# Attention outputs of sixteen units summed inside PSUM, with a drain between row halves, and three weight stores moved to SP

## The chip, the core and the metric

The kernel runs on one core of a Trainium2 chip, as one program. The metric is the device time of one execution in microseconds. The engines are TensorE (PE, with its weight loads shown as PEld), VectorE (DVE), ScalarE (ACT), GpSimd (POOL) and SyncE (SP, which here only issues DMAs). ACT can issue DMAs as well.

## The reference, cut to what matters

```
gamma = 1 - 2 ** (-5 - arange(8));  state = 0
for t in range(768):                                   # 4 batches, 8 heads, head size 64
    state = gamma * state + outer(k[t], v[t])          # one 64x64 state per batch and head
    y[t] = q[t] @ state / sqrt(64)
x = y of all heads side by side                        # 3072 tokens x 512
h = x @ w_in; g = h - tanh(h); x = g @ w_out           # 512 -> 2048 -> 512
h = x @ w_in2; solu, layer norm; out = ln @ w_out2     # 512 -> 1024 -> 512
```

The decay is taken out of the recurrence by scaling q and v with tables of powers of gamma, so that a chunk of 128 tokens needs only matrix products: the output of a chunk is (state before it) times q, plus v times the masked scores inside the chunk.

## The kernel before, in words

The tokens are cut into 24 attention units: 6 chunks `c` of 128 tokens times 4 batches `b`, unit k = 4c + b. Four units make a superblock of 512 tokens. Units 0 to 7 come first and alone (the start of the program). Units 8 to 15 are worked between the steps of the first layer on superblocks 0 and 1. Units 16 to 23 come later, inside the next stage.

A unit has two parts. The score part ("sc" in the rows, written for unit `ks`) makes 16 products of keys with queries and then 16 products that update the state, each 64x64; DVE masks the scores (`pr`) and keeps the states (`sb`, `sa`). The output part ("out", for unit `ko`) makes the output: `fr`, state times q, and `y`, v times masked scores. The function `unit(ko, ks)` issues the output part of one unit and then the score part of a later one; in the start loop ks = ko + 2.

TensorE runs 64x64 products in the four quarters of its array: a product whose operands lie in partitions 0 to 63 uses the upper row half, one with operands in 64 to 127 the lower row half. In the kernel before each `y` product goes to a bank chosen by its row half (`y[ab]`), and each `fr` product to the bank of its own row half (`fr[h]`), so that the two halves never write to the same place. The two terms are then added outside: ACT copies `fr` to `xf` in SBUF (lines 295, 298, 299) and DVE adds `y` in one or two operations (line 303). For units 0 to 7 the result is split into a high part `xh` (ACT, line 341) and a low part `xl` (line 342: one half on DVE, the other on POOL; for unit 7 both on DVE). For units 8 to 15 `xf` is kept.

A step of the first layer, `step_h(n, b)`, is 12 products of 128x512 of weight tile n with the split x of superblock b, called step (n, b) below; ACT and DVE then make g = h - tanh(h). The PE order is the order of the code in this part: step (0,0) after the output part of unit 6, step (1,0) after that of unit 7, then (0,1), (1,1), (2,0), (2,1), (3,0) and so on; from n = 3 a call of `unit` follows each pair of steps. The weights arrive as 64-bit words (`raw`, loaded by SP), and ACT and DVE decode them: `wf` on ACT (line 131), four DVE operations (lines 138 to 145), a high part on ACT (line 154) and a low part on DVE (line 155). The decoded tile is also stored to DRAM (`wfd`), at line 185, from ACT's queue. The order inside each engine's stream, where the code does not pin it, is chosen by a scheduler before the program runs; at run time every engine and every DMA queue works strictly in its order.

Of the kernel before, what the change touches and what calls it, by code (L numbers as in the profile page):

```python
# [26 lines left out]
F32 = mybir.dt.float32  # L27
# [3 lines left out]
ALU = mybir.AluOpType  # L31
# [4 lines left out]
B, H, S, D = 4, 8, 768, 64  # L36
P = 128
DM = H * D
NT = B * S
NP = H // 2  # L40
NC = S // P
NU = NC * B
SB = B * P
# [22 lines left out]
def col(p, h):  # L66

    return h ^ (p & 1)
# [22 lines left out]
def body(ctx: ExitStack, tc, z, w_in, w_out, w_in2, w_out2, g_ln, cst, tab, out):  # L91
# [72 lines left out]
    class Decoder:  # L164
# [59 lines left out]
    def rows(h):  # L224
        return slice(h * D, (h + 1) * D)

    def products(todo):
        for o, a, b in todo:
            pin(nc.tensor.matmul(o, a, b, start=True, stop=True, skip_group_check=True), held[0])  # L229

    def prepare(k, own, wide=False, fixed=True):

# [22 lines left out]
            ), wide and fixed)  # L255
        vs[k] = v

    def unit(ko, ks, hold=False, pool=ps_r, tag="r", opool=ps_r, engs=None, amid=None):

        if ko is not None:
            c, b = divmod(ko, B)
            q, v, po, st = qs.pop(ko), vs.pop(ko), pt.pop(ko), (sa.pop(ko, None), sb.pop(ko))
            w = [opool.tile([P, 2, 4 * D], F32, tag="r", name="out") for _ in range(2)]
            fr = [t[:, 0, :].rearrange("q (i t) -> q i t", i=2) for t in w]
            y = [t[:, 1, :].rearrange("q (h i t) -> q h i t", h=2, i=2) for t in w]

            steps = range(2) if c else (1,)  # L270
            products([
                (
                    fr[h][rows(col(2 * i + odd, h)), i, rows(ab)],
                    st[ab][rows(h), 2 * i + odd, :], q[rows(h), 2 * i + odd, rows(ab)],
                )
                for i in range(2) for ab in steps for odd in range(2) for h in range(2)
            ])
            products([
                (
                    y[ab][rows(col(p, h)), h, p // 2, :], v[rows(ab), 2 * p + h, :],  # L280
                    po[rows(ab), h, p, :],
                )
                for p in range(NP) for ab in range(2) for h in range(2)
            ])
            if hold:
                if b == 0:
                    xf_of[c] = xfp.tile([P, 2, 2, SB], F32, tag=f"xf{c % 2}", name="xf")
                xf = xf_of[c][:, :, :, b * P : (b + 1) * P]
            else:
                xf = t2([P, 2, 2, P], F32, "xf")  # L290
            xa = xf.rearrange("q h i t -> q (h i) t")
            ya = [t.rearrange("q h i t -> q (h i) t") for t in y]
            if c:
                for h in range(2):
                    pin(nc.scalar.copy(xf[:, h, :, :], fr[h]), amid)
            else:
                for h in range(2):
                    pin(nc.scalar.copy(xf[:, h, :, rows(1)], fr[h][:, :, rows(1)]), amid)
                pin(nc.scalar.copy(xa[:, :, rows(0)], ya[0]), amid)
            if amid:  # L300
                amid()
            for ab in steps:
                pin(nc.vector.tensor_tensor(
                    xa[:, :, rows(ab)], xa[:, :, rows(ab)], ya[ab], ALU.add
                ), amid)
            if not hold:
                split_x(c, b, xf, engs or (nc.gpsimd, nc.gpsimd), amid)
        if ks is not None:
            c = ks // B
            kt, kv, v, q = zq.pop(ks)[:, 1, :, :], zv.pop(ks), vs[ks], qs[ks]  # L310
            w = [pool.tile([P, 2, 4 * D], F32, tag=tag, name="sc") for _ in range(2)]
            sc, gn = ([t[:, n, :].rearrange("q (p t) -> q p t", p=NP) for t in w] for n in range(2))
            products([
                (sc[h][rows(ab), p, :], kt[rows(h), p, rows(ab)], q[rows(h), p, rows(ab)])
                for p in range(NP) for h in range(2) for ab in range(2)
            ])
            products([
                (gn[ab][rows(h), p, :], kv[rows(ab), 0, p, rows(h)], v[rows(ab), 2 * p + h, :])
                for p in range(NP) for ab in range(2) for h in range(2)
            ])  # L320
            pr = t2([P, 2, NP, D], F32, "pr")
            for h in range(2):
                pin(nc.vector.tensor_tensor(
                    pr[:, h, :, :], sc[h], mask.unsqueeze(1).to_broadcast([P, NP, D]), ALU.mult
                ), amid)
            pt[ks] = pr
            sb[ks] = stp.tile([P, NP, D], F32, tag="sb", name="sb", bufs=3)
            if c == 0:
                nc.scalar.copy(sb[ks], gn[0])
            else:  # L330
                nc.vector.tensor_tensor(sb[ks], sa[ks], gn[0], ALU.add)
            if c < NC - 1:
                sa[ks + B] = stp.tile([P, NP, D], F32, tag="sa", name="sa")
                nc.vector.tensor_tensor(sa[ks + B], sb[ks], gn[1], ALU.add)

    def split_x(c, b, xf, engs, fixed=False):
        if b == 0:
            xt[c] = [[t4([P, 2, SB], F32R, f"x{n}") for _ in range(2)] for n in "hl"]
        for h in range(2):
            xh, xl = (xt[c][n][h][:, :, b * P : (b + 1) * P] for n in range(2))  # L340
            pin(nc.scalar.copy(xh, xf[:, h, :, :]), fixed)
            pin(engs[h].tensor_tensor(xl, xf[:, h, :, :], xh.bitcast(F32), ALU.subtract), fixed)


    def products_h(s, f, pool, tag):
        ph = pool.tile([P, SB], F32, tag=tag, name="ph")
# [257 lines left out]
    def step_h(n, b):  # L604
        if b == 0:
            g2[n] = t4([P, 2, SB], F32, "g")
        less_tanh(products_h(b, n, ps_y, "y"), g2[n][:, b, :])
# [18 lines left out]
            prepare(k, H // 2, True)  # L626

    for k in range(2 * B):
        both = (nc.vector, nc.gpsimd) if k < 2 * B - 1 else (nc.vector, nc.vector)
        unit(  # L630
            k, k + 2 if k + 2 < 2 * B else None, engs=both,
            amid=lambda: ahead(k + 3), **spare
        )
# [12 lines left out]
    gs = {}  # L646

    def split_g(n):
        g = g2.pop(n)
        gs[n] = [split(g[:, b, :], nc.scalar, nc.vector) for b in range(2)]  # L650

    for n in range(NF1):
        while dec1.at[3] < n + 1:
            dec1.step()
        if n == NF1 - 1:
            split_g(0)
        for b in range(2):
            if n > 1 or b:
                step_h(n, b)

        k = 2 * B + n - LATER
        if 2 * B <= k <= 4 * B:
            unit(k - 1 if k > 2 * B else None, k if k < 4 * B else None, True)
# [480 lines left out]
```

## Time and profile before

| | before |
|---|---|
| median of 3 runs (lowest, highest) | 874.56 us (872.98, 876.18) |
| profiled execution | 874.34 us, span 872.6 us, mean TensorE clock 0.992 |
| busy PE, DVE | 838.4 us (96%), 551.0 us (63%) |
| busy ACT, POOL | 438.6 us (50%), 286.6 us (33%) |

Busy time says which engine is nearly full over the whole program; it doesn't say what limits a given stretch. The profiled execution took 1.74 us outside the span of its instructions. In timeline rows the columns are start and length in us, engine, line, operation, tiles and count; brackets give the idle time just before and what ended it. "issue" is a wait for nothing that the profile shows. The trace counts each 64x64 product in f32 as two records.

### The profile page before, as it was taken

Reading aid. Unit: us, or ns where it says so; the run is one execution under the profiler, and the core shown is the slowest. Engines: PE = TensorE matmul, PEld = TensorE weight load, DVE = VectorE, ACT = ScalarE, POOL = GpSimd, SP = SyncE. Lnnn points to the kernel's source line nnn. Section 1 sums busy time; section 2 is a strip of 40 time slices with the busy share of each in tenths; the row PEclk is TensorE's granted clock in tenths of the full one; section 3 lists DMA queues with packets and bytes.
Section 4 is the critical chain, followed back from the end, with each engine's and each line's share of the span. In section 5 each row is a group of like instructions: output and inputs, shape, how many; then the busy total and the mean of one; then the engine's idle time right before and its main releaser. Section 6 shows DMA issues by size and latency. Waiting matters only on the chain.

```text
span 872.6 us, 16582 instructions
## 1 busy us (share of the span) xinstructions
PE 838.4 (96%) x6488; PEld 691.3 (79%) x6488; DVE 551.0 (63%) x1023; ACT 438.6 (50%) x868; POOL 286.6 (33%) x244
## 2 busy tenths in 40 slices
PE   5799999999999988999999999999999999999997
PEld 4678788788877867888788888887788888888886
DVE  3788975999758678224454977566555555555541
ACT  4655644555555546445443445434655555555442
POOL 4411100160624345343300430234644444444200
PEclk8899999999999999999999999999999999999999
DMA  9657754345899617955766456631211111100001
GB/s 365 251 213 280 272 199 138 118 153 181 301 347 346 230 62 234 412 194 176 275 244 207 155 185 217 190 109 48 86 49 49 49 48 48 45 30 25 21 17 48
DMA packets 66462, 144.34 MB, mean 165 GB/s; under 512 B 6608, under 2 KB 19024, under 8 KB 66384
## 3 DMA queue, kind: packets, MB, share of 16 engines
q1 hardware_dynamic: 58032, 128.28, 41.5%
q10 hardware_dynamic: 8352, 15.00, 4.6%
q8 instruction: 51, 0.84, 0.4%
q14 instruction: 27, 0.22, 0.1%
HBM read 94.50 MB, written 48.76 MB: 164 GB/s over the span
## 4 chain that ended last, share of the span: by engine, by line
PE 81%; DVE 8%; DMA 4%; ACT 3%; issue 2%; SPq 1%; POOL 0%; ACTq 0%; POOLq 0%; DVEq 0%
PE py L378 25%; PE po L966 15%; PE ph L739 14%; PE ph L902 13%; PE ph L353 8%; PE out L229 2%; PE ptr L952 2%; DMA z<-z 2%; PE sc L229 2%; DMA raw<-w_in 1%; DVE wcl L162 1%; DMA wod<-wf 1%; DVE wsum L532 1%; DVE hs L765 0%; DVE wf L145 0%
## 5 line engine op out<-in xcount | busy, mean ns | idle before, releaser
L378 PE MATMUL py<-gp,w 128*128 128x512 f32 x768 | 175.6, 389 | 1.6 <-DVE gp L162 1.6
L378 PEld LDWEIGHTS py<-gp,w 128*128 128x128 f32 x768 | 144.0, 188 | 32.3 <-DVE gp L162 2.0
L966 PE MATMUL po<-w,uh 128*128 128x512 f32 x384 | 118.4, 390 | 0.0
L757 POOL TENSOR_TENSOR hs<-hs,th 128x512 f32<-128x512 f32 x48 | 66.5, 1391 | 94.3 <-ACT th L755 81.2
L966 PEld LDWEIGHTS po<-w,uh 128*128 128x128 f32 x384 | 72.0, 188 | 15.0
L353 PE MATMUL ph<-xh,w 128*128 128x512 f32 x256 | 82.2, 395 | 1.1 <-DVE w L155 1.1
L378 PE MATMUL py<-gh,w 128*128 128x512 f32 x256 | 79.3, 390 | 0.3 <-ACT gh L366 0.3
L494 POOL TENSOR_TENSOR yla<-yl,yha 128x512 fp32r<-128x512 f32 (+1 forms) x24 | 34.4, 1453 | 137.4 <-ACT yha L493 137.4
L966 PE MATMUL po<-w,ul 128*128 128x512 f32 x192 | 74.8, 389 | 0.0
L154 ACT CAST w<-wf 128x512 fp32r<-128x512 f32 x70 | 43.0, 620 | 56.8 <-DVE wf L145 48.8
L902 PE MATMUL ph<-w,yhs 128*128 128x512 f32 x192 | 61.2, 400 | 1.0 <-ACT part L909 1.0
L739 PE MATMUL ph<-xh,wch 128*128 128x512 f32 x140 | 56.8, 405 | 5.3 <-DVE hs L765 4.7
L162 DVE TENSOR_TENSOR gp<-g,gp 128x512 fp32r<-128x512 f32 x64 | 49.7, 788 | 18.8 <-ACT gp L161 18.6
L755 ACT ACTIVATE th<-hs 128x512 f32<-128x512 f32 x48 | 30.3, 631 | 55.3 <-DVE hs L765 51.4
L155 DVE TENSOR_TENSOR w<-wf,w 128x512 fp32r<-128x512 f32 x70 | 50.5, 726 | 11.2 <-ACT w L154 10.2
L353 PEld LDWEIGHTS ph<-xh,w 128*128 128x128 f32 x256 | 48.0, 188 | 12.1 <-DVE w L155 1.5
L378 PEld LDWEIGHTS py<-gh,w 128*128 128x128 f32 x256 | 48.0, 188 | 10.6 <-ACT gh L366 0.7
L739 PE MATMUL ph<-xh,wcl 128*128 128x512 f32 x140 | 54.7, 390 | 0.0
L739 PE MATMUL ph<-xl,wch 128*128 128x512 f32 x140 | 54.6, 390 | 0.0
L765 DVE TENSOR_TENSOR hs<-ph,part 128x512 f32<-128x512 f32 x48 | 32.8, 686 | 34.6 <-PE ph L739 20.4
L927 ACT ACTIVATE ex<-hn,nm 128x1024 f32<-128x1024 f32 x24 | 27.7, 1153 | 53.1 <-DVE nm L917 52.1
L739 PE MATMUL ph<-xh,wc 128*128 128x512 f32 x168 | 52.9, 390 | 1.0 <-DVE hs L765 0.8
(124 smaller groups left out, 1771.5 us busy)
## 6 DMA issues: line engine op xcount, KB each, us to landing
z<-z SPq DMA_DIRECT2D x48, 512.0 KB, 6.9
g<-gd SPq DMA_DIRECT2D x64, 256.0 KB, 5.3
raw<-w_in SPq DMA_DIRECT2D x24, 512.0 KB, 6.4
raw<-w_out SPq DMA_DIRECT2D x24, 512.0 KB, 4.4
gd<-hs SPq DMA_DIRECT2D x48, 256.0 KB, 3.2
y1d<-ysb SPq DMA_DIRECT2D x24, 256.0 KB, 3.4
wc<-wcd SPq DMA_DIRECT2D x12, 512.0 KB, 6.9
yl<-y1d SPq DMA_DIRECT2D x12, 512.0 KB, 3.9
```

The lines of the kernel that those rows point to most:

```text
L154: pin(nc.scalar.copy(hi, wf), fixed)
L155: pin(eng.tensor_tensor(lo, wf, hi.bitcast(F32), ALU.subtract), fixed)
L162: eng.tensor_tensor(o, src, h.bitcast(F32), ALU.subtract)
L229: pin(nc.tensor.matmul(o, a, b, start=True, stop=True, skip_group_check=True), held[0])
L353: nc.tensor.matmul(ph, a[:, k, :], x, start=n == 0, stop=n == 3 * NK - 1), s < 2
L378: nc.tensor.matmul(py[e], a[:, cols], x, start=f == 0 and n == 0, stop=f == NF1 - 1 and n == 2)
L494: nc.gpsimd.tensor_tensor(o, src, h.bitcast(F32), ALU.subtract)
L739: nc.tensor.matmul(ph, a, x, start=first and n == 0, stop=n == 5, skip_group_check=True)
L757: eng.tensor_tensor(g, h, th, ALU.subtract)
L765: nc.vector.tensor_tensor(h, ph, part, ALU.add)
L902: nc.tensor.matmul(ph, x[:, r, :], w, start=first and n == 0, stop=n == 5, skip_group_check=True)
L966: nc.tensor.matmul(po, a[:, f, :], b, start=f == 0 and n == 0, stop=f == NF2 - 1 and n == 2)
```

## The change

For units 0 to 15 the output part goes to a new function `outputs`. Both terms of row half h are accumulated in one bank `w[h]`. The products whose operands lie in the bank's own row half (`fr` and half of `y`, `own(0)`) come first. The other half of `y` (`own(1)`) comes from the opposite row half into the same bank, behind a `drain` of TensorE, in `rest`. `unit` issues `rest` between the score products and the state products of the next unit; where there is no next unit (units 6, 7 and 15) it is returned and issued after the following step. ACT and DVE then read the finished sum from PSUM: `xh` and `xl` directly for units 0 to 7, with `xl` always on DVE, and one copy for each half for units 8 to 15. The DVE additions are gone for these units. Units 16 to 23 keep the old way (`outputs_apart`). The stores of weight tiles 0, 1 and 2 go from ACT's queue to SP's.

```diff
-                        pin(nc.scalar.dma_start(out=to, in_=wf), fixed)
+                        (nc.scalar if i > 2 else nc.sync).dma_start(out=to, in_=wf)
...
+    def outputs(ko, pool, amid):
...
+        w = [pool.tile([P, 2, P], F32, tag="r", name="out") for _ in range(2)]
+        steps = range(2) if c else (1,)
+        def own(off):
+            return [
+                (
+                    w[h][rows(col(p, h)), p // 2, rows(h ^ off)], v[rows(h ^ off), 2 * p + h, :],
+                    po[rows(h ^ off), h, p, :], False,
+                )
+                for p in range(NP) for h in range(2)
+            ]
+        products([
+            (
+                w[h][rows(col(2 * i + odd, h)), i, rows(ab)],
+                st[ab][rows(h), 2 * i + odd, :], q[rows(h), 2 * i + odd, rows(ab)],
+                i == 0 and ab == steps[0],
+            )
+            for i in range(2) for ab in steps for odd in range(2) for h in range(2)
+        ] + own(0))
+        def rest(hold):
+            pin(nc.tensor.drain())
+            products(own(1))
+            if not hold:
+                split_x(c, b, w, amid)
+                return
+            for h in range(2):
+                pin(nc.scalar.copy(xf_to(c)[:, h, :, b * P : (b + 1) * P], w[h]), amid)
...
+        return rest
...
     def unit(ko, ks, hold=False, ...):
...
+        products([(sc[h][...], kt[...], q[...]) ...])
+        if rest:
+            rest(hold)
+        products([(gn[ab][...], kv[...], v[...]) ...])
...
+    def split_x(c, b, w, amid):
...
         for h in range(2):
+            pin(nc.scalar.copy(part[h][0], w[h]), amid)
...
+        for h in range(2):
+            pin(nc.vector.tensor_tensor(
+                part[h][1], w[h], part[h][0].bitcast(F32), ALU.subtract
+            ), amid)
...
             step_h(k - (2 * B - 2), 0)
+            rest(False)
...
             if n > 1 or b:
                 step_h(n, b)
+            if later:
+                later(True)
+                later = None
```

The drain has no row of its own in the listings below, which give the order of an engine's instructions without any time.

TensorE, before: the end of step (0,0) (`ph`), the whole output part of unit 7, and the first product of step (1,0).

```order
L353 MATMUL ph<-xh,w 128x512
L229 MATMUL out<-vq,sa 64x64 x4
L229 MATMUL out<-vq,sb 64x64 x4
L229 MATMUL out<-vq,sa 64x64 x4
L229 MATMUL out<-vq,sb 64x64 x4
L229 MATMUL out<-pr,vq 64x64 x16
L353 MATMUL ph<-xh,w 128x512
```

TensorE, changed, at the same place.

```order
L396 MATMUL ph<-xh,w 128x512
L230 MATMUL out<-pr,vq 64x64 x8
L230 MATMUL out<-vq,sa 64x64 x4
L230 MATMUL out<-vq,sb 64x64 x4
L230 MATMUL out<-vq,sa 64x64 x4
L230 MATMUL out<-vq,sb 64x64 x4
L230 MATMUL out<-pr,vq 64x64 x8
L396 MATMUL ph<-xh,w 128x512
```

The first eight products behind step (0,0) are now the second half of unit 6; the second half of unit 7 has moved behind step (1,0), directly ahead of step (0,1), which reads unit 7's `xh` and `xl`.

SP's DMA queue, before, from the 20th entry, with buffer numbers: `tab` are the q tables, `raw` the weight tiles 2 to 6, `z` the input of later units.

```order
L1016 DMA gl_70<-g_ln 128x8
L208 DMA tab_1061<-tab 128x512
L208 DMA tab_1447<-tab 128x512
L125 DMA raw_931<-w_in 128x1024
L125 DMA raw_933<-w_in 128x1024
L125 DMA raw_978<-w_in 128x1024
L125 DMA raw_980<-w_in 128x1024
L125 DMA raw_1016<-w_in 128x1024
```

SP's DMA queue, changed, at the same place.

```order
L1063 DMA gl_70<-g_ln 128x8
L185 DMA wfd0_71<-wf_286 128x512
L208 DMA tab_1029<-tab 128x512
L185 DMA wfd1_72<-wf_386 128x512
L208 DMA tab_1413<-tab 128x512
L125 DMA raw_886<-w_in 128x1024
L125 DMA raw_888<-w_in 128x1024
L185 DMA wfd2_73<-wf_890 128x512
L125 DMA raw_946<-w_in 128x1024
L125 DMA raw_948<-w_in 128x1024
```

The stores of tiles 0 and 1 stand around a table load, and the store of tile 2, which waits until `wf_890` is decoded, stands ahead of the loads of tiles 4 and later.

DVE, changed, just behind the finish of weight tile 2, with buffer numbers: `wf_950`, `wf_952` and `wf_954` are weight tiles 3, 4 and 5, and `w_964` is the finished tile 3.

```order
L138 TENSOR_SCALAR wf_950<-wf_950 128x512
L138 TENSOR_SCALAR wf_952<-wf_952 128x512
L139 TENSOR_SCALAR wf_950<-wf_950 128x512
L139 TENSOR_SCALAR wf_952<-wf_952 128x512
L138 TENSOR_SCALAR wf_954<-wf_954 128x512
L142 SCALAR_TENSOR_TENSOR wf_950<-raw_888,wf_950 128x512
L142 SCALAR_TENSOR_TENSOR wf_952<-raw_946,wf_952 128x512
L139 TENSOR_SCALAR wf_954<-wf_954 128x512
```

Before, tile 3 was taken through lines 138, 139 and 142 ahead of the first operation on tile 4; now operations on tiles 4 and 5 stand between those on tile 3.

## Rows read from the trace of the kernel before

**Rows 1.** The page: busy time, PE by 40 slices, instruction queue (packets, MB, share).

```profile
PE 838.4 (96%) x6488; PEld 691.3 (79%) x6488; DVE 551.0 (63%) x1023; ACT 438.6 (50%) x868; POOL 286.6 (33%) x244
...
PE   5799999999999988999999999999999999999997
...
q8 instruction: 51, 0.84, 0.4%
```

**Rows 2.** Chain of waits, 0 to 200 us: start, length, what.

```profile
65.89 1.09 PE sc L229 x64
...
128.72 16.56 PE ph L353 x72
```

**Rows 3.** PE in order of time, 20 to 41 us.

```profile
22.37 0.38 PE L229 MATMUL sc<-vq,z 64*64 64x64 f32 x3 [1.89 <-issue]
...
28.13 0.50 PE L229 MATMUL out<-vq,sb 64*64 64x64 f32 x13 [2.22 <-ACT sb L329]
...
29.27 2.05 PE L229 MATMUL sc<-vq,z 64*64 64x64 f32 x63
...
35.96 0.27 PE L229 MATMUL out<-vq,sa 64*64 64x64 f32 x1 [1.00 <-issue]
...
40.31 0.27 PE L229 MATMUL out<-vq,sa 64*64 64x64 f32 x2 [2.22 <-issue]
```

**Rows 4.** DMA queues, stretches of 0.2 us from 19.7, 33.5, 37.9 and 103.6 us.

```profile
q8 instruction: 1, 0.02, 33.8%
...
q8 instruction: 1, 0.02, 30.0%
...
q8 instruction: 1, 0.02, 29.8%
...
q8 instruction: 1, 0.02, 30.2%
```

**Rows 5.** ACT in order of time, 20 to 48 us.

```profile
23.01 0.67 ACT L131 ACTIVATE wf<-raw 128x512 f32<-128x512 f32 x1 [1.83 <-DMA z<-z]
...
27.70 0.37 ACT L329 COPY sb<-sc 128x256 f32<-128x256 f32 x1 [0.52 <-DVE pr L323]
...
46.84 0.71 ACT L341 CAST xh<-xf 128x256 fp32r<-128x256 f32 x2 [0.88 <-DVE xf L303]
```

**Rows 6.** DVE in order of time, 45 to 61 us.

```profile
45.99 0.75 DVE L303 TENSOR_TENSOR xf<-xf,out 128x256 f32<-128x256 f32 x2 [0.46 <-ACT xf L295]
47.27 0.76 DVE L342 TENSOR_TENSOR xl<-xf,xh 128x256 fp32r<-128x256 f32 x2 [0.53 <-ACT xh L341]
...
59.87 0.68 DVE L155 TENSOR_TENSOR w<-wf,w 128x512 fp32r<-128x512 f32 x1
```

**Rows 7.** PE in order of time, 45 to 107 us.

```profile
45.20 0.50 PE L353 MATMUL ph<-xh,w 128*128 128x512 f32 x1
...
60.61 0.73 PE L353 MATMUL ph<-xh,w 128*128 128x512 f32 x2 [1.06 <-DVE w L155]
...
106.01 0.46 PE L229 MATMUL sc<-vs,z 64*64 64x64 f32 x16 [0.60 <-issue]
```

**Rows 8.** Line 229, 64 to 130 us: duration in ns, least, median and most.

```profile
L229 PEld LDWEIGHTS out<-pr,vs x256: 135/135/135, 73.0 to 128.5; 64*64 64x64 f32 x128
L229 PE MATMUL out<-pr,vs x256: 218/218/218, 73.1 to 128.5; 64*64 64x64 f32 x128
```

**Rows 9.** DMA issues to 60 us (KB, us to landing), and SP in order of time.

```profile
raw<-w_in SPq DMA_DIRECT2D x8, 512.0 KB, 7.0
...
36.02 3.25 SPq L125 DMA_DIRECT2D raw<-w_in  x5
```

**Rows 10.** Busy time by stretch: PE, PEld, DVE, ACT, POOL, then clock and DMA.

```profile
128.00:150.00 22.00, 22.00 (x146) 18.28 (x136) 12.26 (x22) 8.44 (x16) 0.00 (x0) 1.00 0.42 137
...
160.00:180.00 20.00, 20.00 (x90) 16.55 (x89) 20.00 (x38) 10.61 (x19) 8.54 (x1) 1.00 0.41 132
```

**Rows 11.** Who PE waited for, 200 to 260 us: total, times, longest.

```profile
PE out L229 <- DVE sa L334: 0.9, 1, 0.9
PE ph L739 <- ACT ysb L388: 0.3, 1, 0.3
```

More of the change, by code (lines that the diff above doesn't have):

```diff
@@ L227, in products @@
     def products(todo):
-        for o, a, b in todo:
-            pin(nc.tensor.matmul(o, a, b, start=True, stop=True, skip_group_check=True), held[0])
+        done = []
+        for o, a, b, *first in todo:
+            done.append(nc.tensor.matmul(
+                o, a, b, start=not first or first[0], stop=True, skip_group_check=True
+            ))
+            pin(done[-1], held[0])
+        return done
     def prepare(k, own, wide=False, fixed=True):
@@ L300, in unit @@
             if amid:
                 amid()
[L302 to L334, printed above, removed]
@@ L336, in split_x, with xf_to, outputs_apart @@
-    def split_x(c, b, xf, engs, fixed=False):
+        return rest
+    def xf_to(c):
+        if c not in xf_of:
+            xf_of[c] = xfp.tile([P, 2, 2, SB], F32, tag=f"xf{c % 2}", name="xf")
+        return xf_of[c]
+    def outputs_apart(ko, pool):
+        c, b = divmod(ko, B)
+        q, v, po, st = qs.pop(ko), vs.pop(ko), pt.pop(ko), (sa.pop(ko, None), sb.pop(ko))
+        w = [pool.tile([P, 2, 4 * D], F32, tag="r", name="out") for _ in range(2)]
+        fr = [t[:, 0, :].rearrange("q (i t) -> q i t", i=2) for t in w]
+        y = [t[:, 1, :].rearrange("q (h i t) -> q h i t", h=2, i=2) for t in w]
+        products([
+            (
+                fr[h][rows(col(2 * i + odd, h)), i, rows(ab)],
+                st[ab][rows(h), 2 * i + odd, :], q[rows(h), 2 * i + odd, rows(ab)],
+            )
+            for i in range(2) for ab in range(2) for odd in range(2) for h in range(2)
+        ])
+        products([
+            (
+                y[ab][rows(col(p, h)), h, p // 2, :], v[rows(ab), 2 * p + h, :],
+                po[rows(ab), h, p, :],
+            )
+            for p in range(NP) for ab in range(2) for h in range(2)
+        ])
+        xf = xf_to(c)[:, :, :, b * P : (b + 1) * P]
+        xa = xf.rearrange("q h i t -> q (h i) t")
+        ya = [t.rearrange("q h i t -> q (h i) t") for t in y]
+        for h in range(2):
+            nc.scalar.copy(xf[:, h, :, :], fr[h])
+        for ab in range(2):
+            nc.vector.tensor_tensor(xa[:, :, rows(ab)], xa[:, :, rows(ab)], ya[ab], ALU.add)
@@ new lines, in unit @@
+    def unit(ko, ks, hold=False, pool=ps_r, tag="r", opool=None, amid=None):
+        rest = None
+        if ko is not None and opool:
+            outputs_apart(ko, opool)
+        elif ko is not None:
+            rest = outputs(ko, ps_r, amid)
+        if ks is None:
+            return rest
+        c = ks // B
+        kt, kv, v, q = zq.pop(ks)[:, 1, :, :], zv.pop(ks), vs[ks], qs[ks]
+        w = [pool.tile([P, 2, 4 * D], F32, tag=tag, name="sc") for _ in range(2)]
+        sc, gn = ([t[:, n, :].rearrange("q (p t) -> q p t", p=NP) for t in w] for n in range(2))
+        products([
+            (sc[h][rows(ab), p, :], kt[rows(h), p, rows(ab)], q[rows(h), p, rows(ab)])
+            for p in range(NP) for h in range(2) for ab in range(2)
+        ])
+        if rest:
+            rest(hold)
+        products([
+            (gn[ab][rows(h), p, :], kv[rows(ab), 0, p, rows(h)], v[rows(ab), 2 * p + h, :])
+            for p in range(NP) for ab in range(2) for h in range(2)
+        ])
+        pr = t2([P, 2, NP, D], F32, "pr")
+        for h in range(2):
+            pin(nc.vector.tensor_tensor(
+                pr[:, h, :, :], sc[h], mask.unsqueeze(1).to_broadcast([P, NP, D]), ALU.mult
+            ), amid)
+        pt[ks] = pr
+        sb[ks] = stp.tile([P, NP, D], F32, tag="sb", name="sb", bufs=3)
+        if c == 0:
+            nc.scalar.copy(sb[ks], gn[0])
+        else:
+            nc.vector.tensor_tensor(sb[ks], sa[ks], gn[0], ALU.add)
+        if c < NC - 1:
+            sa[ks + B] = stp.tile([P, NP, D], F32, tag="sa", name="sa")
+            nc.vector.tensor_tensor(sa[ks + B], sb[ks], gn[1], ALU.add)
@@ L628, in body @@
     for k in range(2 * B):
-        both = (nc.vector, nc.gpsimd) if k < 2 * B - 1 else (nc.vector, nc.vector)
-        unit(
-            k, k + 2 if k + 2 < 2 * B else None, engs=both,
+        rest = unit(
+            k, k + 2 if k + 2 < 2 * B else None,
             amid=lambda: ahead(k + 3), **spare
```

49 lines of the change are left out of this document (10 added, 39 removed).

## The prediction

> **What bounds the kernel now.** I read the page first. PE is busy 96% of the span, and its row of slices falls short only at the start: 5 and 7 tenths in the first two slices of 21.8 us, 9 nearly everywhere after [rows 1]. So there are two programs to cost: a start of about 40 us in which PE waits, and a rest in which PE's own work sets the time. The chain of waits agrees: from 65 us on, its pieces are PE's products one after the other, the score parts of units 8 to 15 among them and then 72 products of steps in 16.56 us, 0.23 us each [rows 2].
>
> In the rest, therefore, work taken from DVE and ACT buys nothing by itself. DVE is idle for almost half of 128 to 150 us, right behind the units that the change relieves, and is full again from 160 us on with other work, while PE is full all the while [rows 10].
>
> In the start, PE's timeline shows who it waits for. One wait of 2.22 us is for ACT's `sb` at 28.13. Three others, 1.89, 1.00 and 2.22 us, carry "issue": nothing that the profile shows [rows 3]. I looked for them in the DMA queues. q8 moves 51 packets of 0.84 MB in all, 16 KB each, and PE executes 6488 products and 6488 weight loads, 254 for each packet [rows 1]: q8 is PE's instruction stream, 127 records of one load and one product to a packet. Counting the records in PE's order, the three waits stand at records 348, 726 and 849, and a later one of 0.60 us at 1864 [rows 7]: distances of 3, 1 and 8 packets within a few records. A packet lies in the stretch that starts 2.7, 2.5, 2.4 and 2.4 us ahead of the four resumptions [rows 4]. I take it that PE stops where its instructions end, and resumes about 2.4 us after the next packet starts. The packets come 1 to 4 us after PE enters the one before, later when the DMA queues are full.
>
> **The change part by part.** *A, the start up to record 849.* ACT's queue loses the store of tile 0, behind which ACT stood 1.83 us for a z load's semaphore before `wf` of tile 1 [rows 5]. Each unit also loses a round trip, ACT `xf`, DVE add, ACT `xh`, DVE `xl`: DVE waits 0.53 us for `xh` in each round, and ACT 0.88 for the addition [rows 5, 6]. Worked along the engines' orders, the `sb` that released PE at 28.13 was written by ACT at 27.70 [rows 3, 5] and comes about 2 us sooner. But PE then meets the next packet boundary, record 474, ten records into the output part of unit 3. Its packet comes behind the z loads as before, and PE reached that record at 28.3. So nothing is won there. Up to record 600 the score part runs 63 records in 2.05 us, half of the speed of 64 in 1.09 later [rows 2, 3], which makes 126 records 4 us, no less than before, and a drain is added. At 726 and 849 the instructions are late again, at 35.96 and 40.31 [rows 3]. The five raw loads that SP issued at 36.02 [rows 9] are now two, issued near 29.5, and no longer fill the queues ahead of the packet for record 849. I count a gain of 0.25 us at that record (bounds: 1.2 gained, 0.9 lost, a packet's spread).
>
> *B, from there to the third product of step (3,0).* Before, this ran from 40.31 to 60.61 with one wait of 1.06 us for `w` of tile 3 [rows 3, 7]. Added are two drains and a new wait. The second half of unit 7 now stands behind step (1,0) and directly ahead of step (0,1), so PE waits for its result: the product's end (0.22 us), ACT's first `xh` (about 0.4 of the pair's 0.71), then DVE's first `xl` (0.4 of 0.76) for the second product, less one product of 0.23: 0.9 us [rows 2, 5, 6, 8]. Before, the pair of `xl` at 47.27 was just in time and PE did not wait. Queued behind PE's wait are all the steps. DVE loses four additions here, two for each of units 6 and 7 (0.75 us for a pair [rows 6]). But tile 3 now waits for loads: SP's store of tile 2 stands until that tile is decoded, near 48 us, and the loads of tiles 4 and 5 start behind it. They land 4.5 to 6 us later (the median is 7.0 in a fuller queue [rows 9]), and DVE's order ties tile 3 to them. I get tile 3 finished at about 60 us, before at 60.55 [rows 6], against a need at 61. So the old wait of 1.06 goes, and B costs 2 drains + 0.9 - 1.06.
>
> *A drain's price.* No row shows one. Records follow each other every 17 ns (64 in 1.09 us [rows 2]); at a drain PE has to see the last product end, 218 ns, and the next weight load, 135 ns, can't be started early [rows 8]. Without any restart it costs 0.218 - 0.015 = 0.20 us, with the whole load exposed 0.34, with a further 0.25 for the sequencer 0.6. A lower end of 0.15 holds if the modelled end of a product is late. I take 0.34, since the load ahead of its product is what rolling hides. The Trainium skill (PSUM — Partial Sum Buffer, Engine vs sequencer instructions) says that a drain waits until the engine is fully idle, and its page on TensorE (TensorE: Matmul & The Clock Gate, Single matmul latency) gives (398 + N)/2.4 ns for one product, 192 ns at N = 64, an estimate near the row's 218; by it alone the ten drains behind record 849 would cost 1.9 us. So B is 0.68 + 0.9 - 1.06 = +0.5 us.
>
> *C, units 8 to 15.* The products are as many as before. Eight drains stand in a stretch where PE never waits: 8 x 0.34 = +2.7 us (1.2 to 4.8). The removed additions and the changed copies were hidden behind PE. If that cover were gone, they would be worth 8 x 0.75 = 6 us, but the rows of 60 to 130 us show PE waiting 0.60 us in all, for instructions.
>
> *D, given back later.* PE waits 0.9 us for DVE's `sa` and 0.3 for ACT between 200 and 260 us [rows 11], at the end of a chain of loads that DVE and SP set. A PE that comes later waits less there: -0.4 us (0 to -1.2).
>
> The sum is -0.25 + 0.5 + 2.7 - 0.4 = +2.6 us on the profiled 874.34: 876.9 us. That execution lies 0.2 us from the median of the runs, so the same number stands for both.
>
> **The rivals.** *The start comes free (the other side).* If the "issue" waits are no fixed instruction supply and move with the dependences, record 849 comes when the data allow. The shorter rounds then take PE there at about 35 instead of 40.3 us, 5.2 us sooner, while the loads for tile 3 move up as well: 876.9 - 5.2 = 871.7 us. For it speak the 1.83 us of ACT and the rounds of 2.6 to 3 us between units, which PE's work alone would fill in 2. Against it stand the packets ahead of all four resumptions. It decides once the start gains more than 2.6 us. The Trainium skill (Runtime: NRT & Kernel Launch, Instruction fetch mechanics) has instructions refilled in blocks of 16 KiB, as q8 shows, and says that this fetch is hidden by the issue floor. By that rule the rival would hold; the four waits here disagree with it.
>
> *Cheap drains.* At 0.20 us each, C is 1.6 and B 0.24, and the time 875.5 us. For it speaks that a record's length is the only wait that must be; against it, that nothing can load weights ahead of a drain.
>
> *SP's queue holds the weights up.* If the loads behind the store of tile 2 take the 7.0 us of the row, or the decode of tile 2 is 1 to 2 us late, tile 3 is done near 63 us and PE waits 2 us in step (3,0): 878.9 us. Queued behind that store are all later raw and z loads, and ACT's and DVE's decode waits for them. Against it: the queue is far emptier then than at 36 us.
>
> **How the numbers follow.** Forecast 0.40, start free 0.27, cheap drains 0.18, SP's queue 0.15. About 0.3% (2.6 us) is what a measurement of this kernel can tell from no change, so "the same" runs from 871.9 to 877.2. The forecast lies near its upper edge: half of it and a little of the cheap drains count as slower, with most of the last case (0.38 in all). The start coming free lies on the lower edge and gives faster 0.15, other gains 0.02 (0.17 in all). The rest is 0.45. The range, 871.5 to 880.0, goes from that rival to drains of 0.6 us with SP's wait. The likeliest case's own range is 875 to 879.
>
> **What would show it.** In the changed profile: PE's "issue" waits still at the packet boundaries, with packets about 2.4 us ahead, and the resumption in unit 6's output near 40 us (wrong if it is below 38); a gap of about 0.9 us ahead of the first products of step (0,1), released by ACT or DVE; no wait for `w` in step (3,0), which starts near 60.5; a gap between the score records and the next `out<-pr` records in each of units 8 to 15, of 0.34 us from start to start (wrong below 0.2); and PE's waits between 200 and 260 us smaller. The prediction fails most simply if the start's waits are shorter than the packets say, or if the drain is nearly free.

## The result and the profile after

| | before | after |
|---|---|---|
| median (lowest, highest) | 874.18 us (872.98, 876.18) | 881.39 us (880.17, 882.98) |
| profiled execution, span | 872.6 us | 879.4 us |
| busy PE, DVE, ACT, POOL | 838.4, 551.0, 438.6, 286.6 us | 843.6, 546.6, 433.0, 282.8 us |

The change makes the kernel slower: ratio 1.0077, 95% interval 1.0055 to 1.0099, about 6.7 us. The forecast was 876.9 us with a range up to 880.0.

PE's timeline from 20 to 45 us answers to [rows 3]:

```profile
22.42 0.38 PE L230 MATMUL sc<-vq,z 64*64 64x64 f32 x4 [2.29 <-issue]
26.99 0.34 PE L230 MATMUL out<-vq,sb 64*64 64x64 f32 x7 [0.96 <-ACT sb L368]
29.25 0.49 PE L230 MATMUL out<-vq,sb 64*64 64x64 f32 x9 [1.92 <-issue]
33.78 0.27 PE L230 MATMUL out<-vq,sa 64*64 64x64 f32 x2 [0.78 <-issue]
37.91 0.28 PE L230 MATMUL out<-vq,sa 64*64 64x64 f32 x3 [1.61 <-issue]
41.74 0.38 PE L230 MATMUL out<-vq,sa 64*64 64x64 f32 x4 [0.46 <-issue]
```

The wait for ACT's `sb` fell from 2.22 to 0.96 us, and the time went into waits for instructions: the five "issue" waits stand behind 345, 471, 597, 723 and 849 records of products in the trace, each 126 further on. The place of the product that started at 40.31 is now reached at 41.74.

PE from 45 to 80 us answers to [rows 7]:

```profile
45.41 0.39 PE L396 MATMUL ph<-xh,w 128*128 128x512 f32 x1
45.91 0.46 PE L230 MATMUL out<-pr,vq 64*64 64x64 f32 x16
...
50.13 0.46 PE L230 MATMUL out<-pr,vq 64*64 64x64 f32 x16
51.06 0.50 PE L396 MATMUL ph<-xh,w 128*128 128x512 f32 x1 [0.47 <-ACT xh L380]
51.82 0.50 PE L396 MATMUL ph<-xl,w 128*128 128x512 f32 x1 [0.26 <-DVE xl L384]
52.16 0.62 PE L396 MATMUL ph<-xh,w 128*128 128x512 f32 x2
...
64.03 0.73 PE L396 MATMUL ph<-xh,w 128*128 128x512 f32 x2 [0.80 <-DVE w L155]
...
69.24 0.69 PE L230 MATMUL sc<-qs,z 64*64 64x64 f32 x32
69.97 2.01 PE L230 MATMUL sc<-vs,z 64*64 64x64 f32 x32
...
78.32 0.66 PE L230 MATMUL sc<-qs,z 64*64 64x64 f32 x32
79.10 0.46 PE L230 MATMUL out<-pr,vs 64*64 64x64 f32 x16
```

Four things are to be seen. Behind a step, the drain shows as 0.50 us from the last `ph` to the first `out` (0.32 before). Step (0,1) waits at 51.06 and 51.82 for the x of unit 7. The wait for `w` of tile 3, 1.06 us before, is still there with 0.80. And the score part of unit 8 takes from 69.24 to 71.91, 2.67 us, where it took 1.10: its products come one by one, as ACT writes the scaled v (`vs`).

Why `w` and `vs` are late is read first from ACT's timeline:

```profile
54.65 0.60 ACT L403 ACTIVATE th<-ph 128x512 f32<-128x512 f32 x1 [2.85 <-PE ph L396]
55.15 1.93 ACT L131 ACTIVATE wf<-raw 128x512 f32<-128x512 f32 x3
...
69.20 0.33 ACTq L185 DMA_DIRECT2D wfd<-wf  x1
69.57 2.02 ACT L253 ACTIVATE vs<-z,con 128x64 f32<-128x64 f32 x8 [2.39 <-DVE wf L145]
```

The same two operations of ACT in the kernel before:

```profile
63.25 2.02 ACT L248 ACTIVATE vs<-z,con 128x64 f32<-128x64 f32 x8
67.24 0.33 ACTq L185 DMA_DIRECT2D wfd<-wf  x1
```

DVE's first operation on tile 3, before and then changed:

```profile
53.50 0.42 DVE L138 TENSOR_SCALAR wf<-wf 128x512 f32<-128x512 f32 x1
```

```profile
55.89 0.94 DVE L138 TENSOR_SCALAR wf<-wf 128x512 f32<-128x512 f32 x2
```

The chain of waits gives the same from PE back to PE (start, length, what; compare [rows 2]):

```profile
51.82 2.81 PE ph L396 x11
55.25 1.12 ACT wf L131 x2
...
62.28 1.71 DVE w L155
64.03 5.28 PE ph L396 x22
...
71.98 5.66 PE ph L396 x24
...
128.38 5.66 PE ph L396 x24
```

ACT's first decode operation for tiles 3, 4 and 5 (`wf`, line 131) stands in its queue behind `th` of step (0,1). PE reached that step late, so ACT stood 2.85 us, and DVE, with nothing to decode, 2.59 us. DVE starts on tile 3 at 55.89 where it started at 53.50, and is done at 63.97 (before 60.55 [rows 6]): the decode itself takes 8.08 us where it took 7.05, with operations on tiles 4 and 5 now between those on tile 3. The lateness of unit 8 has to do with ACT's order. Its `vs` now stands behind the store at 69.20, which by its place in the queue is that of tile 6 and waits for DVE to decode that tile; ACT stood 2.39 us there. In the kernel before, `vs` stood ahead of that store. From 71.98 to 128.38 there are seven rounds of a unit and two steps: 8.06 us each. Before they were 7.76, without the 0.60 us wait of [rows 7].

After less before at six places: +1.43 us at the product of [rows 3] (40.31), +3.42 at the third product of step (3,0), +4.99 behind unit 8's scores, +6.97 at 156 us (where 163.43 answers to 156.46), +6.80 at 336 us and +6.80 at the end of the span.

### The profile page after: what moved, and what is told of

Read it like the earlier page. It is cut to its first block, busy times and chain, and to the rows that moved or that the text cites. A ratio compares the mean times of both kernels' runs of the same rounds, so it can differ in the third digit from the quotient of the medians.

```text
span 879.4 us, 16525 instructions
## 1 busy us (share of the span) xinstructions
PE 843.6 (96%) x6488; PEld 694.3 (79%) x6488; DVE 546.6 (62%) x1002; ACT 433.0 (49%) x848; POOL 282.8 (32%) x237
## 4 chain that ended last, share of the span: by engine, by line
PE 78%; DVE 12%; issue 4%; DMA 3%; ACT 2%; SPq 0%; POOL 0%; ACTq 0%; DVEq 0%; POOLq 0%
PE py L421 19%; PE ph L786 15%; PE po L1013 15%; PE ph L949 13%; PE ph L396 9%; PE out L230 3%; PE sc L230 3%; DMA z<-z 2%; PE ptr L999 2%; DVE gl L412 1%; DVE wf L142 1%; DVE w L155 1%; DVE wcl L162 1%; DVE wf L145 1%; DVE wf L138 1%
## 5 line engine op out<-in xcount | busy, mean ns | idle before, releaser
L155 DVE TENSOR_TENSOR w<-wf,w 128x512 fp32r<-128x512 f32 x70 | 52.0, 747 | 12.2 <-ACT w L154 10.9
```

The lines of the kernel that those rows point to most:

```text
L155: pin(eng.tensor_tensor(lo, wf, hi.bitcast(F32), ALU.subtract), fixed)
```

## Experiments

The ratios are against the kernel before, run on the same chip beside each; 0.1% is 0.87 us. Medians of the kernel before were 875.1 to 875.5 us there, single runs 871.7 to 880.8, so an interval is some 1.5 us wide to either side. Not all runs were made beside each other, so two of them are better compared by their ratios than by their medians. Traces drift apart behind 156 us, too, where no edit reaches: in one run below, the loads held in the kernel before, PE is 0.89 us behind the kernel before at 156 us and 3.37 at the end. Of this, 1.6 us come at 335 to 340 us, where the granted clock fell to half (1.2 GHz) just after PE had resumed from a wait of 2.01 us; it stayed at full (2.4 GHz) in the kernel before, behind a wait of 2.03 at the same place. One thing more holds for these runs: the scheduler orders ACT and DVE anew for each edited kernel, and in most of them it changed these orders.

**The three stores back on ACT.** On the changed kernel:

```diff
-                        (nc.scalar if i > 2 else nc.sync).dma_start(out=to, in_=wf)
+                        pin(nc.scalar.dma_start(out=to, in_=wf), fixed)
```

> The changed kernel with the stores of weight tiles 0, 1 and 2 back on ACT's queue; the orders of PE and DVE are untouched. Theory A (SP's queue is a main cost): in the changed kernel the store of tile 2 went out at 50.13 us and the raw and z loads behind it only then. With the store gone from SP the loads of tiles 4 to 6 go out near 31 us, PE's wait of 0.80 us for w in step (3,0) disappears, and the records of unit 8's score part take 1.1 us instead of 2.67: 2.0 to 2.5 us less, about 879. Theory B (drains and late second halves alone): the loads have slack, at most 0.5 us less, about 881. ACT's wait of 1.8 us for the store's semaphore near 21 us comes back; if instructions bound the start, record 849 moves by less than 0.7 us for it.

Measured: 885.38 us, 1.0104 (1.0072 to 1.0136), slower than with the stores on SP by 4.0 us of the medians and 2.4 by the ratios, whose intervals overlap. PE's timeline:

```profile
39.93 0.37 PE L230 MATMUL out<-vq,sa 64*64 64x64 f32 x3 [4.08 <-issue]
44.02 0.28 PE L230 MATMUL out<-vq,sa 64*64 64x64 f32 x4 [0.25 <-issue]
```

The busy time from 30 to 40 us, with columns as in [rows 10]:

```profile
30.00:40.00 10.00, 5.28 (x224) 4.63 (x218) 6.15 (x19) 3.99 (x16) 0.58 (x1) 0.84 0.91 325
```

Both theories expected less. SP issued the loads of tiles 2 to 6 from 30.0 to 33.8 us (36.0 to 39.3 before [rows 9]), the DMA engines were 91% busy, and PE stood 4.08 us for a packet. The weights wait of step (3,0) fell to 0.28 us, but unit 8's scores took as long as in the changed kernel (2.68 us), with DVE's order the same and `vs` behind tile 6's store as there. So unit 8 is late without a store on SP as well; and by holding the loads that store spares the start some 2 us (41.74 against 44.02).

**The stores alone on SP,** in the kernel before (the same line the other way).

> The kernel before with only the stores of tiles 0, 1 and 2 on SP. Theory A: the store of tile 2 holds SP until that tile is decoded near 51 us, unit 8's z and the raw loads of tiles 4 to 6 come after it, PE waits in step (3,0) for 2 to 3 us instead of 1.06 and in unit 8's score part 1 to 1.5 us more: 2 to 3.5 us slower, 876.5 to 878. Theory B: no change beyond 0.5 us, since the loads have slack. If dependences rather than instructions bound the start, ACT's 1.8 us come off and record 849 is resumed near 38.5 instead of 40.31.

Measured: 880.05 us, 1.0054 (1.0032 to 1.0075), more than expected. In the old order tile 2 is decoded later, its store goes out at 53.44 us, and the loads behind it follow. ACT, which waits for one of them:

```profile
58.08 0.66 ACT L131 ACTIVATE wf<-raw 128x512 f32<-128x512 f32 x1 [2.96 <-DMA raw<-w_in]
```

PE in the same run:

```profile
69.52 2.16 PE L229 MATMUL sc<-vs,z 64*64 64x64 f32 x32 [1.45 <-ACT vs L248]
```

Here the rival of SP's queue is real: ACT waits 2.96 us for a raw tile, and unit 8 is late. The place where PE pays is unit 8, not step (3,0). Some 1.3 us of the loss stand ahead of all this: the product of [rows 3] started at 41.63.

**The second half of units 6 and 7 ahead of their steps,** in the changed kernel; all other code as it is.

```diff
     for k in range(2 * B):
...
+        if rest:
+            rest(False)
...
             step_h(k - (2 * B - 2), 0)
-            rest(False)
```

> The changed kernel with the drain and second half of units 6 and 7 put back ahead of steps (0,0) and (1,0), as the output parts stood before; the stores stay on SP. Theory (the second half of unit 7 directly ahead of step (0,1) makes PE wait for xh and xl): the gaps at 51.06 and 51.82 us go, 1.2 to 1.7 us sooner at the third product of step (0,1); but step (3,0) then waits that much longer for w, which comes when the loads behind the store of tile 2 allow, so the total falls by 0 to 0.8 us only, 880.5 to 881.4. Rival (the waits are independent): the full 1.5 us off, 879.8.

Measured: 878.03 us, 1.0026 (1.0009 to 1.0043), 3.4 us below the changed kernel by the medians, 4.5 by the ratios, and 4.2 in the traces at 156 us. PE:

```profile
66.22 0.69 PE L230 MATMUL sc<-qs,z 64*64 64x64 f32 x32
66.74 0.93 PE L230 MATMUL sc<-vs,z 64*64 64x64 f32 x32
```

The wait for x, the wait for `w` and the slow scores of unit 8 are all gone, though the store on SP still stands until 50.69 us. The place of `rest`, behind the step, with the orders that the scheduler makes of it, is the largest single loss, more than twice the most that was expected of it.

The edit moves products of PE alone, but the scheduler then ordered DVE and ACT otherwise as well. DVE's first and last operation on tile 3, and ACT's `vs` of unit 8 with tile 6's store:

```profile
53.97 0.42 DVE L138 TENSOR_SCALAR wf<-wf 128x512 f32<-128x512 f32 x1
...
59.31 0.68 DVE L155 TENSOR_TENSOR w<-wf,w 128x512 fp32r<-128x512 f32 x1
```

```profile
65.26 2.02 ACT L253 ACTIVATE vs<-z,con 128x64 f32<-128x64 f32 x8
67.70 0.33 ACTq L185 DMA_DIRECT2D wfd<-wf  x1
```

DVE takes tile 3 ahead of most of tiles 4 and 5 again and needs 6.02 us for it, not 8.08; `vs` is ahead of the store again. So this run shows what the whole edit is worth, not what the wait for x is worth alone.

**Eight drains alone,** in the kernel before, between the score and the state products of units 8 to 15.

```diff
+            if hold:
+                pin(nc.tensor.drain())
             products([(gn[ab][...], ...) ...])
```

> The kernel before with nothing but a drain added between the score products and the state products of units 8 to 15, eight in all. Theory (a drain costs what the gaps of the changed kernel show): each period between two output parts grows from 7.75 by 0.30 us, 2.4 us in all, 876.6; the wait of 0.60 us at 105 us may go. Rival (cheap drains, the cost lies in splitting the output part): under 0.1 us each, 874.2 to 875.

Measured: 880.17 us, 1.0048 (1.0027 to 1.0069). The chain:

```profile
70.34 5.66 PE ph L355 x24
78.51 5.66 PE ph L355 x24
```

The round is 8.17 us, 0.41 more than before; eight of them are 3.3 us, the interval of the ratio is 2.4 to 6.0. Its product of [rows 3] started at 41.80, though nothing ahead of it differs from the kernel before: the five loads were issued at 36.02 in both, but PE resumed on the packet before at 36.35 and not at 35.96, and the next one started at 39.56 and not at 37.95. The granted clock then stood at half (1.2 GHz) from 40.5 to 47.3 us, a stretch that began within PE's wait of 3.32 us for that packet. So this trace is 2.88 us behind at step (3,0), ahead of the first added drain, and its time holds more than the drains.

**Forty drains ahead of the first product,** in the kernel before, which move every record behind them by 20.

```diff
+    for _ in range(40):
+        pin(nc.tensor.drain())
```

> The kernel before with 40 drains of TensorE put ahead of its first matrix product, which lengthens the program by 20 records of the kind that a 64x64 product counts as two of, and changes nothing behind them. If the waits put down as 'issue' in the first 45 us are waits for the next packet of instructions, they move by those 20 records: they stand ahead of records 328, 452, 577, 706 and 829 of the products' own count (348, 471, 597, 723 and 849 before), so the last of them falls ahead of the second half of the unit's products and no longer ahead of the first product of a step. If they have another cause that the profile does not name (a queue, the weights, the clock), they stay at the same records as before. Time within 2 us of the kernel before by both.

One execution, 877.31 us. PE's timeline:

```profile
21.99 0.62 PE L229 MATMUL sc<-vq,z 64*64 64x64 f32 x26 [2.29 <-issue]
28.02 0.44 PE L229 MATMUL sc<-vq,z 64*64 64x64 f32 x11 [1.94 <-issue]
...
32.10 0.37 PE L229 MATMUL out<-vq,sa 64*64 64x64 f32 x3 [0.51 <-issue]
...
40.48 0.29 PE L229 MATMUL out<-vq,sa 64*64 64x64 f32 x5 [2.37 <-issue]
46.52 0.45 PE L229 MATMUL out<-pr,vq 64*64 64x64 f32 x12 [0.97 <-issue]
```

The first four stand behind 326, 453, 579 and 832 records, within three of the forecast. At the fifth place of the forecast, behind 706, PE waits 1.44 us too, but the profile puts that down to DVE. The last, behind 960, is one packet further on and falls inside a unit's `out<-pr` run. So these "issue" waits are the instruction supply.

**New outputs in units 0 to 7 only,** the second half first, stores on SP (the kernel of 878.03 us with units 8 to 15 in the old way):

```diff
-            later = unit(..., True)
+            unit(..., True, opool=ps_r)
```

> The changed kernel with the second row half of units 6 and 7 ahead of their steps, as in the run before, and with units 8 to 15 in the old manner (both terms in banks of their own, no drain); stores 0 to 2 on SP. If the eight drains of units 8 to 15 cost 0.30 us each up to the end, the time is that of the run before less 2.4: 875.6. Rival: they are given back later in the program, and the time stays at 878. The period between the units after 75 us should be 7.75 us, as in the kernel before, by both.

Measured: 876.81 us, 1.0014 (0.9999 to 1.0029): 1.2 us for units 8 to 15 (1.0 by the ratios), of the 2.4 that eight rounds show.

**New outputs in units 8 to 15 only,** in the kernel before: `outputs` and `later` of the change for these units, `xf` and the additions for units 0 to 7.

> The kernel before with units 8 to 15 alone in the new manner (both terms in one bank, the second row half behind the scores and a drain); stores 0 to 2 on ACT, units 0 to 7 as before. If the drains are the whole of it, period 8.05 against 7.75 and 2.4 us more than the kernel before: about 877. Rival: what the eight drains alone cost in an otherwise unchanged kernel (about 5 us in the timed comparison, 3.3 by the periods) is what they cost here too: 878.5 to 880. If the accumulation in place gives time back (two copies and two additions fewer for each unit), 874.5 to 876.

Measured: 877.33 us, 1.0025 (1.0007 to 1.0043), with rounds of 8.06 us: +1.8 us. Both runs put this part of the change at 1 to 2 us, a little below the drains' own 2.4.

**As the run with units 0 to 7 new, stores on ACT:** the line of the first experiment.

> As the kernel with units 0 to 7 alone in the new manner, but with stores 0 to 2 on ACT, so that the loads of tiles 2 to 6 go out some 15 us earlier. If the stores on SP cost what they hold back (weights of step (3,0), block z of unit 8), this is 2 us faster than with them on SP: about 873.5. If the loads that they hold back are what delays the packets of instructions (the last issue wait in the first 45 us ended at 44.0 with all stores on ACT, at 41.7 with three on SP), this is slower by 2 to 4 us: about 878.

Measured: 881.09 us, 1.0068 (1.0045 to 1.0091), 4.3 us slower than with the stores on SP. PE in this kernel:

```profile
40.20 0.28 PE L230 MATMUL out<-vq,sa 64*64 64x64 f32 x3 [3.81 <-issue]
```

Its busy time from 35 to 38 us, the last two columns being the DMA share and GB/s:

```profile
35.00:38.00 3.00, 1.30 (x68) 1.15 (x68) 1.97 (x6) 1.60 (x6) 0.00 (x0) 1.00 1.05 421
```

PE in the kernel with the stores on SP:

```profile
37.47 0.28 PE L230 MATMUL out<-vq,sa 64*64 64x64 f32 x3 [1.33 <-issue]
41.31 0.28 PE L230 MATMUL out<-vq,sa 64*64 64x64 f32 x4 [1.33 <-issue]
```

And its busy time in the same stretch:

```profile
35.00:38.00 3.00, 1.67 (x102) 1.52 (x102) 2.08 (x6) 1.60 (x6) 0.00 (x0) 1.00 0.07 23
```

The product at 40.20 is the one at 37.47 there: with the DMA engines full, its packet started at 37.7 instead of 35.2 us. The second experiment on the stores thus agrees with the first. Not all of the 4.3 us is the packets' part: at the end of unit 8's scores the two traces are 4.65 us apart, 2.96 from ahead of these scores and 1.69 from within them, where `vs` stands behind tile 6's store with the stores on ACT and ahead of it with them on SP.

**The same with the five loads held:** the kernel with stores on ACT, and a transfer of 512 bytes on SP that reads the x of unit 6, ahead of the loads.

```diff
                 dec1.to(0, 4)
+                nc.sync.dma_start(out=scr, in_=xt[1][0][0].bitcast(F32)[:, 0, 2 * P : 2 * P + 1])
```

> As the run before with units 0 to 7 alone in the new manner and all stores on ACT, and one transfer of 512 bytes on SP's queue ahead of the loads of tiles 2 to 6, which waits for the x of unit 6 and so holds those five loads from 30 us to about 42. If these loads are what delays the packets of instructions, the packets start as with three stores on SP (35 and 39 us, not 37.6 and 41.9), the last issue wait of the first 45 us ends near 41.3, and the time is 875 to 877 against 881.1 with the loads at 30 us. Rival: the loads do nothing to the packets, the issue waits stay where they were, and tiles 2 and 3 come later on top: 881 to 884.

Measured: 878.58 us, 1.0035 (1.0018 to 1.0051), 2.5 us below, with intervals that just overlap. The loads went out at 44.2. PE:

```profile
41.93 0.28 PE L230 MATMUL out<-vq,sa 64*64 64x64 f32 x4 [1.60 <-issue]
68.37 2.16 PE L230 MATMUL sc<-vs,z 64*64 64x64 f32 x32 [0.91 <-ACT vs L253]
```

The packets start at 35.3 and 39.2 us, as forecast: it is the loads that delay them. But unit 8 waits 0.91 us here and 0.88 in the run before, with `vs` behind tile 6's store in both, and the forecast had left that out; so 878.6, not 875 to 877. The profiled execution was the slowest of this kernel, 881.59 us.

**The loads held in the kernel before,** with the same transfer.

> The kernel before with the same small transfer ahead of the loads of tiles 2 to 6, which go out at about 43 us and not at 36.0. If the loads delay the packets, the packet that started at 37.9 starts near 36.5 and the product that waited for it (40.31) starts 1 us earlier; behind that tile 3 has 7 us less in hand and its weights may come up to 2 us later for step (3,0). Sum: 874 to 877. Rival: no effect on packets, so only the lateness of the tiles shows: 877 to 880.

Measured: 876.18 us, 1.0007 (0.9991 to 1.0024): no difference. The packet starts at 37.97, with the loads at 36.0 at 37.95, and the product behind it at 40.38 (40.31 before). In the trace of before the loads came just too late to hinder it; in that of the eight drains they did not, and the packet came 1.6 us later. My expectation of 1 us failed.

**Only the loads of tiles 4 to 6 held,** those of tiles 2 and 3 pinned ahead of the transfer.

> As the run with the five loads held until 44 us (878.6 measured), but only those of tiles 4 to 6 are held; tiles 2 and 3 are loaded at 30 us, as they are with three stores on SP. If the loads at 30 us delay the packets only when all five go, the packets start at 35 and 39 us and the last issue wait of the first 45 us ends near 41.3; tiles 2 and 3 are then in hand, unit 8 waits for nothing, and the time is 875 to 877. Rival: two loads are enough to delay the packets, 43 to 44 us and 879 to 881. If it is 873 or less it beats the kernel before, which rests on 875.5 in these runs.

Measured: 878.40 us, 1.0034 (1.0017 to 1.0051). The packets do as forecast, at 34.6 and 38.5, and the product starts at 40.79. Unit 8 does not: its scores take 2.49 us, one by one behind `vs`, which stands behind tile 6's store again:

```profile
66.17 2.01 PE L232 MATMUL sc<-vs,z 64*64 64x64 f32 x32
```

The profiled execution took 877.63 us. At 156 us its trace is 1.36 us behind the kernel before, and that of the run with the stores on SP 1.32; the difference of the medians, 878.4 to 876.8, is within the intervals. It does not beat the kernel before.

**Four drains for one** in units 8 to 15, in the kernel of 878.03 us.

> The changed kernel with the second row half of units 6 and 7 ahead of their steps (878.0 measured), and with four drains in a row in place of one in each of units 8 to 15. If the price of a drain is the emptying of TensorE's pipeline, the three further ones find it empty and cost almost nothing: period at most 0.1 us over 8.05, time 878 to 879. Rival: each drain costs its own 0.30 us: period 8.95, time 885.

Measured: 881.04 us, 1.0062 (1.0037 to 1.0087). PE:

```profile
91.00 0.66 PE L230 MATMUL sc<-qs,z 64*64 64x64 f32 x32
91.97 0.46 PE L230 MATMUL out<-pr,vs 64*64 64x64 f32 x16 [0.31 <-issue]
```

From scores to outputs 0.97 us against 0.78 with one drain; the round grew from 8.05 to 8.29. Three further drains cost about 0.08 us each: between the two theories, nearer to the first. By this, some 0.22 of a lone drain's 0.30 us is the emptying of the pipeline. The time grew by 3.0 us, eight rounds by 1.9; at 156 us the two traces are 2.4 us apart.

## Why the prediction was wrong, step by step

**The step that failed is B's "So the old wait of 1.06 goes".** I had tile 3 finished at about 60 us, whenever PE came; it was finished at 63.97, and PE waited 0.80 us for it. I priced B at +0.5; it measured +2.0, and unit 8, for which the sum had no term, another +1.57. I had seen that PE would wait for the x of unit 7, and sized that nearly right: 1.1 us against 0.9, whose own terms make 0.8 (from 50.13, the three starts at 51.06, 51.82 and 52.16 would have been 50.48, 50.82 and 51.05).

I left out two things. The decode of tile 3 follows PE: its `wf` stands on ACT behind `th` of step (0,1). In all eight kernels with the new outputs in units 0 to 7, DVE's first operation on tile 3 starts 3.70 to 3.77 us behind the third product of that step (52.16 to 55.89 in the changed one). Whatever makes PE late, the wait for x included, makes tile 3 as late. And DVE's order, with tiles 4 and 5 between the operations on tile 3, makes that decode 8.08 us long. PE needs 10.9 us from the third product of step (0,1) to that of step (3,0), so a decode of more than about 7.2 us makes it wait.

The run with the second half first takes all three waits away, but one wait did not draw the others after it. The wait for x goes with the place of `rest`. The decode of tile 3 starts as far behind PE there as in the changed kernel (3.70 us); the wait for `w` goes since DVE's order takes 6.02 us. Unit 8 follows ACT's order. In five kernels `vs` stands behind tile 6's store, and unit 8's scores take 2.49 to 3.69 us, though three of the five have no wait for x. In the eight others they take 1.09 to 1.99 us, and in one more, the stores alone on SP, 4.24, since loads are late. No run changed these orders alone, so this split of the 3.4 us rests on the traces.

**The rival of SP's queue** came nearest in time (878.9), in part by luck. Its condition came true: the store of tile 2 went out at 50.13 us, where I had 48, and tile 3 was done near 64. But with the stores on ACT again, and the loads out at 30 us, unit 8 was as late and `w` still waited 0.28 us, so only some 0.5 us of the wait for `w` can be the queue's. In the old order the mechanism exists (the stores alone: 880.05 us). In the run with the second half first ACT stands 1.26 and 0.91 us for two of these loads, in the changed kernel for none, as it comes to them later.

**A, the start.** The waits stayed at the packet boundaries, as forecast, and the rival of a start that comes free is out: 41.74 where it needed 35. The shift of 20 records shows the supply. The size was off: -0.25 forecast, +1.43 in the profiles, outside my bounds. Part of that is the trace of before: with the same early order on PE and the stores on ACT, four traces have this product at 39.67, 40.31, 40.38 and 41.80 us (the second of them before, the third with the loads held), so one trace could not give the term to better than about 1 us. These four have a mean of 40.54, and four traces with the new early order and three stores on SP (41.19, 41.31, 41.40 and 41.74) one of 41.41: a loss of 0.87 us, at the edge of my bounds, and of the other sign than forecast. That the loads no longer fill the queues ahead of a packet was right, but with a meaning that I missed. The new outputs take POOL's part of the split away, SP's table load, which waited for POOL until 35.6 us, goes out at 29.3 to 29.6, and all five raw loads would follow into the packets. The third store on SP holds three of them back, and so prevents a loss that the rest of the change makes: 2.4 and 4.7 us by the ratios of the two pairs of runs, some of it at unit 8 and not at the packets.

**The drain.** 0.34 us forecast each; 0.30 by the round in units 8 to 15, 0.18 behind a step of large products. No run shows the 0.25 us for the sequencer in my upper bound; a drain that finds PE empty cost about 0.08. C was forecast at +2.7; from unit 8's end to 156 us it measured +1.98, the 0.60 us wait for instructions at 106 us having gone. The rival of cheap drains is out in its place, and right behind the steps.

**D** was forecast at -0.4; -0.17 was given back: PE's wait for `sa` was 1.0 us against 0.9, and only the 0.3 for ACT went. The parts now sum to 1.43 + 1.99 + 1.57 + 1.98 - 0.17 = 6.80, the spans' difference. Of B's 1.99, two drains (0.36) and the x wait (1.1) less the shorter `w` wait (0.26) make 1.2; of the other 0.8, about half goes with the granted clock, which stood at half (1.2 GHz) from 39.3 to 42.6 us, behind PE's wait of 1.61 us at 37.91, and at full (2.4 GHz) in the kernel before: 31 records took 1.10 us where 44 took 0.92. The rest I can't assign to a row.

**What stays open:** what DVE's and ACT's orders cost by themselves; why eight drains in the old order cost 0.41 us a round and 0.30 in the new one, and why the part in units 8 to 15 shows 1.2 us in one pair of runs and 1.8 in the other, which the intervals don't separate.

## What to carry to other kernels

When an edit puts a new wait on one engine, write down what is queued behind the consumer of the waiting result on each other engine, to the next place where the first engine needs them; here tile 3 started 3.7 us behind step (0,1), however late that step came. Compare also the orders of all engines around the edit, before and after: in these traces the wait for `w` and the slow scores of unit 8 went with the orders of DVE and ACT, and not with the wait that the edit itself made. When an edit frees an engine early in a program, look at which DMA waits for that engine, and whether the transfer that it lets go meets the instruction packets. Of the versions tried none beat the kernel before; the best of the new ones, only units 0 to 7 summed in PSUM, is 1.0014 (0.9999 to 1.0029).

## What the runs showed of the hardware

**Instruction packets.** Where the DMA engines have little else to move (a busy share of at most 0.06 from 36 to 42 us), PE's next packet of 16 KB starts 1.3 to 1.6 us after PE resumes on the one before, and PE resumes 2.2 to 2.8 us after that: 3.6 to 4.1 us from one resumption to the next in six of these traces (37.47 to 41.31 and 37.91 to 41.74 among them), for 126 records that PE could work off in 2.2 us (64 take 1.09, [rows 2]). With five loads of 512 KB in the way (a share of 0.88 to 1.04 from 33.5 to 42 us) it was 6.3 and 6.6 us (33.87 to 40.20, 33.33 to 39.93). The Trainium skill (Runtime: NRT & Kernel Launch, Instruction fetch mechanics) describes the refills in blocks of 16 KiB and calls them hidden; these waits disagree with the second half of that.

**Drains.** Between 64x64 products a drain costs 0.30 us (0.78 from the scores' start to the next products), behind 128x512 products 0.18, and each further one in a row about 0.08. In the kernel before, between scores and state products, it cost 0.41 a round.
